# Three slots for block 1's diagonal products, quarter copies of W_in, and one cast moved to VectorE

## The chip, the cores and the metric

The kernel runs on one core of one Trainium2 chip. The metric is the device time of one execution in microseconds (us). The time stamps below are us from the start of the profiled span; a profile is one execution, and the span is some 1.8 us shorter than the time reported for it.

## The reference

```python
# causal depthwise convolution over the sequence, softmax-normalised weights per head, 7 taps
w = softmax(weight)                                   # [8 heads, 7]
out[b, s, h, :] = sum_k w[h, k] * x_pad[b, s + k, h, :]   # x: [8, 4096, 192]
# then a two-layer perceptron with exact GELU on the 32768 tokens
h = out.reshape(32768, 192) @ w_in                    # w_in: [192, 2048]
g = 0.5 * h * (1 + erf(h / sqrt(2)))
y = g @ w_out                                         # w_out: [2048, 192]
```

## The kernel before

The tokens go through in blocks: six of 256 columns, then blocks of 512, each for both halves of the tokens. Names used below: PE is TensorE, ACT is ScalarE, DVE is VectorE, POOL is GpSimd.

The 192 channels are held as three planes of 64. For blocks 0 and 1 the convolution is done on PE, as products with diagonal matrices accumulated in PSUM (`pconv`, 7 taps for each of four groups `kd`: planes 0 and 1, and two halves of plane 2). From block 2 on it is done on DVE. The evictions of block 1's products, that is the copies out of PSUM to `xc`, are on DVE. A part below is the share of one plane in the first products of a unit; `S_PCE` has counted two evictions of block 0 already, hence the 2:

```python
def wait_pc(e, n, p):               # block 1: parts 0, 1, 2 need 1, 3, 6 of the six evictions
    if n == 0: ...
    else:
        e.wait_ge(S_PCE, 2 + (1, 3, 6)[p])
```

DVE's program at the start, and PE's for block 0 (a "unit" is one call of `mm1`, 12 first-layer products that one GELU of ACT consumes; block 0 has units 0 to 7):

```python
for p in range(NP):                 # DVE
    trans(0, p)
conv_out(v, 0, 1)
conv_out(v, 0, 4)
dup(0)                              # copies of W_in to the other 64 partitions,
dup(1)                              # needed by units 4, 5, 6
for p in range(NP):
    trans(1, p)
dup(2)                              # twice as long as the others
for j in range(len(PIECES)):        # six evictions of block 1
    conv_out(v, 1, j)
# ... cut: transposes and taps of block 2 and on

behind = {                          # PE: block 1's diagonal products, each set in a slot behind a unit of block 0
    (0, 4): [(1, kd, k) for k in taps for kd in (0, 1)],
    (0, 5): [(1, kd, k) for k in taps for kd in (2, 3)],
}
def mm1(n, i):
    if u >= 2:
        t.wait_ge(S_GELU, u - 1)    # two PSUM buffers between PE and ACT
    if i == 0:
        if n in PC: wait_pc(t, n, NP - 2)
        else: t.wait_ge(S_CV, cvd(n))   # block 2 and on wait for DVE's convolution
    # ... cut: waits for W_in and its copies
    for cc in range(c):
        for p in range(NP):
            if n in PC and i == 0 and cc == 0 and p == NP - 1:
                wait_pc(t, n, p)    # the third part waits for all six evictions
            # ... cut: the products
```

The second layer of block 0 (`mm2`) starts behind block 1's first unit. I call the start of its first product the *hand-over*.

Of the kernel before, what the change touches and what calls it, by code (L numbers as in the profile page):

```python
# [11 lines left out]
def bass_lightweight_conv__then__act_gelu_exact_kernel(  # L12
# [9 lines left out]
    D2, F = moe_w_in.shape  # L22
# [10 lines left out]
    WS = [256] * 6 + [512] * ((HALF - 1536) // 512)  # L33
    PC = {0: 0, 1: 1}
# [7 lines left out]
    NP = D // 64  # L42
# [6 lines left out]
    HX = 8  # L49
    HF = HX - (KS - 1)  # L50
    XW = HX + TB
    HB = KS - 1
    HL = 32 * HB
    XB = HL + WS[0]
# [36 lines left out]
    for n in range(NB):  # L91
        k = 64 if n == 0 or M0 <= n < M1 else 16 * NG[n] if n < NB - 1 else 32 * NG[n]
# [10 lines left out]
    def sem(name):  # L103
        return es.enter_context(nc.semaphore(name))

    def ap(t, off, pat):
        return bass.AP(t, off, pat)

    with es:
        win = sbt("win", [128, NP * F], BF16)  # L110
# [14 lines left out]
        xTb = [sbt("xTb%d" % i, [128, NP * XB], BF16) for i in range(len(PC))]  # L125
        xin = [sbt("xin%d" % i, [128, TB // 32 * DQ], F32) for i in range(NX)]
        xT = [sbt("xT%d" % i, [128, NP * XW], F32) for i in range(2)]
# [18 lines left out]
        S_DG = sem("S_DG")  # L146
        S_HOT = sem("S_HOT")
        S_CAST = [sem("S_CAST%d" % i) for i in range(len(PC))]
        S_PC = sem("S_PC")
        S_PCE = sem("S_PCE")  # L150
        S_PCA = sem("S_PCA")
# [2 lines left out]
        S_TR = sem("S_TR")  # L154
# [50 lines left out]
        FQ = F // 8  # L205
# [256 lines left out]
        def _(v):  # L462
# [34 lines left out]

            def dup(s):

                v.wait_ge(S_WIN[s], 32)  # L500
                for hf in range(2):
                    v.tensor_copy(
                        ap(
                            win,
                            64 * (1 - hf) * NP * F + FH + FP[s],
                            [[NP * F, 64], [F, NP], [1, FP[s + 1] - FP[s]]],
                        ),
                        ap(
                            win,
                            64 * hf * NP * F + FP[s],  # L510
                            [[NP * F, 64], [F, NP], [1, FP[s + 1] - FP[s]]],
                        ),
                    ).then_inc(S_DUPE)

            def trans(n, p):
                w = WS[n]
                if p == 0:
                    if xin_at(n) > 0:
                        v.wait_ge(S_XIN[n % NX], xin_at(n))
                    if n >= 2 and n - 2 in PC:  # L520
                        wait_pc(v, n - 2, NP - 1)
                    elif n >= 2:
                        v.wait_ge(S_CV, cvd(n - 2))
                    if n >= 1:
                        v.wait_ge(S_HALO, HC[n])
                v.transpose(  # L526
                    ap(xT[n % 2], p * XW + HX, [[NP * XW, 128], [1, w]]),
                    ap(
                        xin[n % NX],
                        p,  # L530
                        [[TB // 32 * DQ, 128], [D if n == 0 else DQ, w // 32], [NP, 32]],
                    ),
                ).then_inc(S_TR)
# [45 lines left out]

            for p in range(NP):  # L580
                trans(0, p)
            conv_out(v, 0, 1)
            conv_out(v, 0, 4)
            dup(0)
            dup(1)
            for p in range(NP):
                trans(1, p)
            dup(2)
            for j in range(len(PIECES)):
                conv_out(v, 1, j)  # L590

# [17 lines left out]
        @block.scalar  # L609
        def _(a):  # L610
            a.activation(
                out=hot[:, 0:1], in_=nc.const_aps.tensor(0.0, (1, 1), F32), func=AF.Exp
            ).then_inc(S_ACTP)
            load(a, 0, (2, 3))
            a.wait_ge(S_ACTP, 1)
            a.wait_ge(S_PRO, 1)
            a.activation(
                out=wex[:, :],
                in_=wsb[:, :],
                func=AF.Exp,  # L620
                bias=wmx[:, 0:1],
                accum_out=wsm[:, 0:1],
            ).then_inc(S_ACTP)
            a.activation(
                out=hot[:, 1:2], in_=nc.const_aps.tensor(0.0, (1, 1), F32), func=AF.Gelu
            ).then_inc(S_HOT)
            a.wait_ge(S_PRO, 9)
            for p in range(NP):
                a.wait_ge(S_TR, p + 1)  # L629
                a.activation(  # L630
                    out=ap(xTb[0], p * XB + HL, [[NP * XB, 128], [1, WS[0]]]),
                    in_=ap(xT[0], p * XW + HX, [[NP * XW, 128], [1, WS[0]]]),
                    func=AF.Copy,
                ).then_inc(S_CAST[0])
            for j in PA:
                conv_out(a, 0, j)

            due = {(1, 6): [(0, 0)]}
            for m in range(NA):
                if m >= 1:  # L640
                    due[m + 1, NSL[m + 1] // 2] = [(m, 0)]
                due[m + 2, 0] = [(m, 1)]

            first = {}
            for n, at in ((4, (3, 5, 6)), (5, (3, 5, 6)), (6, (2, 3, 5))):
                for p in range(NP):
                    first[n - 2, at[p]] = (n, p)

            def first_tap(n, p):
                w = WS[n]  # L650
                a.wait_ge(S_TR, NP * n + p + 1)
                if p == 0:
                    a.wait_ge(S_CV, cvd(n - 2))
                a.activation(  # L654
                    out=acc[n % 2][:, p * TB : p * TB + w],
                    in_=ap(xT[n % 2], p * XW + HX, [[NP * XW, 128], [1, w]]),
                    func=AF.Copy,
                    scale=wcol[:, KS - 1 : KS],
                ).then_inc(S_K0)

            for n in range(NB):
                w = WS[n]
                for i in range(NSL[n]):
                    u = SL0[n] + i
                    c = NCH[n]
                    if (n, i) in first:
                        first_tap(*first[n, i])
                    for k in due.get((n, i), []):
                        evac(a, *k)
                    a.wait_ge(S_MM1, u + 1)  # L670
                    if i == 0 and n >= 2:
                        a.wait_ge(S_MM2, MMC[n - 1])
                    if M0 <= n < M1:

                        src = [[2 * TB, 128], [1, 2 * TB]]
                        dst = [[NF * 2 * TB, 128], [1, 2 * TB]]
                    else:

                        src = [[2 * TB, 128], [TB, 2], [128, 4], [1, 128]]
                        dst = [[NF * 2 * TB, 128], [128, 2], [256, 4], [1, 128]]  # L680
                    a.activation(  # L681
                        out=ap(gT[n % 2], i * c * 2 * w, dst),
                        in_=ap(hp[u % 2], 0, src),
                        func=AF.Gelu,
                    ).then_inc(S_GELU)

            for g in range(NG[NB - 1]):
                evac_half(a, g, 1)
                store_half(a, g, 1)

        @block.tensor
        def _(t):
            t.wait_ge(S_WARM, 1)
            for i in range(16):
                t.matmul(hp[1][:, 0:512], warm[:, 0:128], warm[:, :])  # L695

            def pconv(n, kd, k):

                p, ex, c0, w = kinds(n)[kd]
                if k == KS - 1:  # L700
                    t.wait_ge(S_CAST[PC[n]], p + 1)
                    if n == 0:
                        t.wait_ge(S_DG, 1)
                if k == KS - 2:
                    t.wait_ge(S_HALO, HC[n] + 2 + p if n == 0 else HC[n + 1])
                for hf in range(2):
                    ho = hf ^ ex
                    r = slice(64 * hf, 64 * hf + 64)
                    d0 = k * 64
                    x0 = p * XB + (32 * k if n == 0 else HF + k) + c0  # L710
                    ins = t.matmul(  # L711
                        bank(kd, slice(64 * ho, 64 * ho + 64), w),
                        dg[r, d0 : d0 + 64],
                        xTb[PC[n]][r, x0 : x0 + w],
                        start=(k == KS - 1),
                        stop=(k == 0),
                        tile_position=(64 * hf, 64 * ho),
                    )
                if k == 0:
                    ins.then_inc(S_PC)  # L720

# [4 lines left out]
            for kd in order:  # L726
                pconv(*seq[kd].pop(0))

            behind = {
                (0, 4): [(1, kd, k) for k in taps for kd in (0, 1)],  # L730
                (0, 5): [(1, kd, k) for k in taps for kd in (2, 3)],
            }

            def mm1(n, i):
# [8 lines left out]
                        t.wait_ge(S_CV, cvd(n))  # L743
                if n == 0 and i < 3:
                    t.wait_ge(S_WIN[i], 32)
                if n == 0 and 4 <= i < 7:
                    t.wait_ge(S_DUPE, 2 * (i - 4) + 2)
                for cc in range(c):
                    for p in range(NP):
# [170 lines left out]
```

## Time and profile before

| | before |
|---|---|
| time, first three runs | 683.58, 683.60, 684.46 us |
| profiled run: time, span | 683.38, 681.6 us |
| PE busy | 675.0 us, 99% |
| DVE, ACT busy | 561.0 and 537.3 us |

PE is busy for 99% of the span. The edits touch only what comes ahead of block 2, so what they change counts only if it reaches PE's first product of block 2. The prediction below shows most of the lines. In them, the third column is the engine, L760 is a first-layer product or its weight load, L711 a diagonal product, L791 a second-layer product of the first blocks, L681 a GELU, L193 a DVE eviction of the convolution, L502 a copy of W_in, L526 a transpose of x and L559 a tap of DVE's convolution. Three more lines are needed below, the start of block 0's transposes, the hand-over and the first product of block 2:

```profile
5.93 1.33 DVE L526 STREAM_TRANSPOSE xT<-xin 128x256 f32<-128x256 f32 x3 [0.68 <-DMA xin<-in_x_dram]
...
18.68 0.49 PE L791 MATMUL ob<-wout,gT 64*128 64x192 bf16 x8
...
29.18 0.83 PE L760 MATMUL hp<-xc,win 64*128 64x256 bf16 x12
```

### The profile page before, as it was taken

Reading aid. Unit: us, or ns where it says so; the run is one execution under the profiler, and the core shown is the slowest. Engines: PE = TensorE matmul, PEld = TensorE weight load, DVE = VectorE, ACT = ScalarE, POOL = GpSimd, SP = SyncE. Lnnn points to the kernel's source line nnn. Section 1 sums busy time; section 2 is a strip of 40 time slices with the busy share of each in tenths; the row PEclk is TensorE's granted clock in tenths of the full one; section 3 lists DMA queues with packets and bytes.
Section 4 is the critical chain, followed back from the end, with each engine's and each line's share of the span. In section 5 each row is a group of like instructions: output and inputs, shape, how many; then the busy total and the mean of one; then the engine's idle time right before and its main releaser. Section 6 shows DMA issues by size and latency. Waiting matters only on the chain.

```text
span 681.6 us, 27317 instructions
## 1 busy us (share of the span) xinstructions
PE 675.0 (99%) x12576; PEld 410.1 (60%) x12576; DVE 561.0 (82%) x904; ACT 537.3 (79%) x550; POOL 38.9 (6%) x57
## 2 busy tenths in 40 slices
PE   8999999999999999999999999999999999999998
PEld 4899655555555555555555555555555555555556
DVE  6899979888889888899888898888898888988611
ACT  6899988787787777787777788777878777878772
POOL 5026000000000000000000000000000000000000
PEclk9999999999999999999999999999999999999999
DMA  9446323234332244332244422334322434310123
GB/s 222 86 101 134 79 60 75 43 75 95 96 94 58 45 91 94 95 86 47 60 94 95 94 69 46 78 94 96 94 52 46 95 94 96 83 42 21 48 49 94
DMA packets 132994, 54.79 MB, mean 80 GB/s; under 512 B 126480, under 2 KB 132752, under 8 KB 132880
## 3 DMA queue, kind: packets, MB, share of 16 engines
q1 hardware_dynamic: 130960, 51.50, 32.5%
q8 instruction: 98, 1.61, 1.0%
q0 software_dynamic: 1248, 0.79, 0.9%
q10 hardware_dynamic: 672, 0.76, 0.4%
q14 instruction: 16, 0.13, 0.1%
HBM read 28.66 MB, written 25.17 MB: 79 GB/s over the span
## 4 chain that ended last, share of the span: by engine, by line
PE 96%; ACT 2%; DMA 1%; issue 0%; DVE 0%; SPq 0%; ACTq 0%
PE hp L760 48%; PE ob L824 43%; PE ob L791 6%; ACT gT L681 2%; DMA xin<-in_x_dram 1%; PE ob L711 0%; ACT xc L191 0%; ACT osb L269 0%; DVE osb L311 0%; DVE xT L526 0%; ACT xTb L630 0%; SPq L872 0%; DVE osb L280 0%; SPq L329 0%; ACTq L629 0%
## 5 line engine op out<-in xcount | busy, mean ns | idle before, releaser
L681 ACT ACTIVATE gT<-hp 128x1024 bf16<-128x1024 f32 x512 | 523.3, 1024 | 128.8 <-PE hp L760 125.5
L760 PE MATMUL hp<-xc,win 64*64 64x512 bf16 (+2 forms) x6048 | 419.5, 366 | 1.5 <-ACT gT L681 0.7
L824 PE MATMUL ob<-gT,wout 64*64 64x512 bf16 x5376 | 366.3, 376 | 0.0
L559 DVE SCALAR_TENSOR_TENSOR acc<-xT,wcol,acc 128x512 f32<-128x512 f32 (+1 forms) x495 | 314.1, 698 | 0.0
L760 PEld LDWEIGHTS hp<-xc,win 64*64 64x64 bf16 (+1 forms) x6048 | 189.9, 106 | 134.8 <-ACT gT L681 2.5
L824 PEld LDWEIGHTS ob<-gT,wout 64*64 64x64 bf16 x5376 | 172.3, 118 | 122.8
L311 DVE STREAM_TRANSPOSE osb<-ob 128x512 f32<-128x512 f32 x84 | 74.1, 885 | 100.8 <-PE ob L824 100.8
L526 DVE STREAM_TRANSPOSE xT<-xin 128x512 f32<-128x512 f32 (+1 forms) x105 | 78.6, 797 | 3.8 <-DMA xin<-in_x_dram 3.8
L559 DVE SCALAR_TENSOR_TENSOR xc<-xT,wcol,acc 128x512 bf16<-128x512 f32 (+1 forms) x99 | 65.0, 708 | 0.0
L447 POOL COPY xT<-xT 128x18 f32<-128x18 f32 x30 | 27.9, 930 | 505.2 <-DVE xT L526 482.9
L791 PE MATMUL ob<-wout,gT 64*128 64x192 bf16 x1024 | 52.9, 243 | 0.3
L791 PEld LDWEIGHTS ob<-wout,gT 64*128 64x128 bf16 x1024 | 44.9, 94 | 5.2 <-PE ob L791 0.6
L552 DVE TENSOR_SCALAR acc<-xT,wcol 128x512 f32<-128x512 f32 (+1 forms) x90 | 37.5, 474 | 1.1
L282 ACT ACTIVATE osb<-ob 128x192 f32<-128x192 f32 x4 | 1.3, 332 | 9.5 <-PE ob L791 9.5
L280 DVE COPY osb<-ob 128x192 f32<-128x192 f32 x4 | 1.4, 358 | 8.4 <-PE ob L791 8.4
L695 PE MATMUL hp<-warm 128*128 128x512 bf16 x16 | 5.1, 485 | 1.3 <-DVE warm L463 1.3
L269 ACT ACTIVATE osb<-ob 128x384 f32<-128x384 f32 x12 | 5.8, 486 | 0.0
L654 ACT ACTIVATE acc<-xT,wcol 128x256 f32<-128x256 f32 (+1 forms) x9 | 5.2, 575 | 0.0
L695 PEld LDWEIGHTS hp<-warm 128*128 128x128 bf16 x16 | 1.8, 119 | 4.0 <-issue 1.9
L384 POOL DMA_DIRECT2D win<-in_moe_w_in_dram x6 | 3.9, 658 | 0.8 <-POOLq L905 0.8
L711 PE MATMUL ob<-xTb,dg 64*64 64x256 bf16 (+1 forms) x112 | 3.2, 245 | 0.7 <-ACT xTb L630 0.7
L193 DVE CAST xc<-ob 64x256 bf16<-64x256 f32 (+3 forms) x8 | 2.8, 357 | 1.3 <-PE ob L711 1.1
(31 smaller groups left out, 22.4 us busy)
## 6 DMA issues: line engine op xcount, KB each, us to landing
out_dram<-osb SPq DMA_DIRECT2D x122, 192.0 KB, 3.1
xin<-in_x_dram SPq DMA_DIRECT2D x116, 192.0 KB, 4.1
xin<-in_x_dram SPq DMA_DIRECT2D x20, 96.0 KB, 4.2
woutf<-in_moe_w_out_dram SPq DMA_DIRECT2D x4, 384.0 KB, 6.2
win<-in_moe_w_in_dram POOLq DMA_DIRECT2D x4, 96.0 KB, 4.6
win<-in_moe_w_in_dram POOLq DMA_DIRECT2D x2, 192.0 KB, 5.1
out_dram<-osb SPq DMA_DIRECT2D x8, 48.0 KB, 1.9
out_dram<-osb ACTq DMA_DIRECT2D x4, 96.0 KB, 1.9
```

Of the source, the lines that this page charges most:

```text
L269: e.activation(out=dst, in_=src, func=AF.Copy).then_inc(S_EVA)
L311: v.transpose(ap(osb[m % 2], j, [[8 * C, 128], [C // 2, TB // 32], [NP, 32]]), bank(ring(m, j)),).then_inc(S_EV)
L447: g.tensor_copy(dst, src).then_inc(S_HALO)
L526: v.transpose(ap(xT[n % 2], p * XW + HX, [[NP * XW, 128], [1, w]]), ap(xin[n % NX], p, [[TB // 32 * DQ, 128], [D if n == 0 else DQ, w // 3 ...
L552: ins = v.tensor_scalar(a, src, wk, None, ALU.mult)
L559: ins = v.scalar_tensor_tensor(dst, src, wk, a, op0=ALU.mult, op1=ALU.add)
L654: a.activation(out=acc[n % 2][:, p * TB : p * TB + w], in_=ap(xT[n % 2], p * XW + HX, [[NP * XW, 128], [1, w]]), func=AF.Copy, scale=wcol[ ...
L681: a.activation(out=ap(gT[n % 2], i * c * 2 * w, dst), in_=ap(hp[u % 2], 0, src), func=AF.Gelu,).then_inc(S_GELU)
L695: t.matmul(hp[1][:, 0:512], warm[:, 0:128], warm[:, :])
L760: ins = t.matmul(hp[u % 2][fo : fo + fw, o : o + w], ap(win, f1, [[NP * F, 64], [2, fw]]), xc[n % 2][r, p * TB : p * TB + w], start=(p == ...
L791: ins = t.matmul(bank(bb[sub], w=C), gT[m % 2][r, c0 : c0 + 128], wout[r, CH[sub][i] * C : (CH[sub][i] + 1) * C], start=(ph == 0 and i == ...
L824: ins = t.matmul(bank(ring(m, j), slice(64 * h, 64 * h + 64), w), ap(wout, 64 * hf * NF * C + CH[h][i] * C + j, [[NF * C, 64], [NP, 64]],) ...
```

## The change

Its intent is to keep ACT fed in block 0: there, ACT stood idle 0.63 and 0.26 us ahead of two GELUs (I call such a gap a bubble). The prediction puts the first down to PE's diagonal products behind unit 4 and the second to a unit that waits for the long copy; the second reading did not hold, as the run with the old slots shows. Four edits:

```diff
-            for i in range(16):                      # warm products on PE
+            for i in range(12):
...
             for p in range(NP):                      # DVE
                 trans(0, p)
+            v.wait_ge(S_TR, NP)
+            v.tensor_copy(<xTb[0], plane 2>, <xT[0], plane 2>).then_inc(S_CASTV)
             conv_out(v, 0, 1)
             conv_out(v, 0, 4)
-            dup(0)
-            dup(1)
+            for s in range(3):                       # dup(s) is now a quarter, FQ columns
+                dup(s)
             for p in range(NP):
                 trans(1, p)
-            dup(2)
+            dup(3)
...
-            for p in range(NP):                      # ACT: casts of block 0
+            for p in range(NP - 1):
...
             behind = {
-                (0, 4): [(1, kd, k) for k in taps for kd in (0, 1)],
-                (0, 5): [(1, kd, k) for k in taps for kd in (2, 3)],
+                (0, 5): [(1, kd, k) for k in taps[:4] for kd in (0, 1)],
+                (0, 6): [(1, kd, k) for k in taps[4:] for kd in (0, 1)],
+                (0, 7): [(1, kd, k) for k in taps for kd in (2, 3)],
             }
...
-                if n == 0 and 4 <= i < 7:
+                if n == 0 and i >= 4:
                     t.wait_ge(S_DUPE, 2 * (i - 4) + 2)
```

(The diff is cut: the addresses of the copies and of the cast, and the semaphore waits that go with the cast, are left out or shortened.)

More of the change, by code (lines that the diff above doesn't have):

```diff
@@ L148, in bass_lightweight_conv__then__act_gelu_exact_kernel @@
         S_CAST = [sem("S_CAST%d" % i) for i in range(len(PC))]
+        S_CASTV = sem("S_CASTV")
         S_PC = sem("S_PC")
@@ L498, in dup @@
             def dup(s):
-                v.wait_ge(S_WIN[s], 32)
+                v.wait_ge(S_WIN[min(s, 2)], 32)
                 for hf in range(2):
@@ L504, in dup @@
                             win,
-                            64 * (1 - hf) * NP * F + FH + FP[s],
-                            [[NP * F, 64], [F, NP], [1, FP[s + 1] - FP[s]]],
-                        ),
-                        ap(
-                            win,
-                            64 * hf * NP * F + FP[s],
-                            [[NP * F, 64], [F, NP], [1, FP[s + 1] - FP[s]]],
-                        ),
+                            64 * (1 - hf) * NP * F + FH + FQ * s,
+                            [[NP * F, 64], [F, NP], [1, FQ]],
+                        ),
+                        ap(win, 64 * hf * NP * F + FQ * s, [[NP * F, 64], [F, NP], [1, FQ]]),
                     ).then_inc(S_DUPE)
@@ L581, in _ @@
                 trans(0, p)
+            v.wait_ge(S_TR, NP)
+            v.tensor_copy(
+                ap(xTb[0], (NP - 1) * XB + HL, [[NP * XB, 128], [1, WS[0]]]),
+                ap(xT[0], (NP - 1) * XW + HX, [[NP * XW, 128], [1, WS[0]]]),
+            ).then_inc(S_CASTV)
             conv_out(v, 0, 1)
             conv_out(v, 0, 4)
-            dup(0)
-            dup(1)
+            for s in range(3):
+                dup(s)
             for p in range(NP):
                 trans(1, p)
-            dup(2)
+            dup(3)
             for j in range(len(PIECES)):
@@ L700, in pconv @@
                 if k == KS - 1:
-                    t.wait_ge(S_CAST[PC[n]], p + 1)
+                    if n == 0 and p == NP - 1:
+                        t.wait_ge(S_CASTV, 1)
+                    else:
+                        t.wait_ge(S_CAST[PC[n]], p + 1)
                     if n == 0:
```

## The prediction

> **What bounds the kernel now.** I read the page first, then the list of waits, the chain of waits, and the timeline of the first 40 us, narrowed to single instructions where two events lie close.
>
> The page says that TensorE is the engine and that the rest of the chain is thin:
>
> ```profile
> PE 675.0 (99%) x12576; PEld 410.1 (60%) x12576; DVE 561.0 (82%) x904; ACT 537.3 (79%) x550; POOL 38.9 (6%) x57
> ...
> PE 96%; ACT 2%; DMA 1%; issue 0%; DVE 0%; SPq 0%; ACTq 0%
> ```
>
> The list of waits for PE alone has five rows, 3.2 us together, and all of them lie in the first 18 us. So everything that the change touches (warm-up, the convolution of blocks 0 and 1 as diagonal products on PE, the copies of W_in across the partition halves) lies in a preamble of about 20 us out of 681.6 us, and from there to the end PE issues back to back, apart from a ScalarE-paced stretch at 70 to 80 us. A shift of PE at 20 us therefore arrives at the end one for one, unless another wait takes it up in between. The question is whether the shift survives until PE is alone. This is the timeline, in four pieces:
>
> ```profile
> 13.79 1.99 DVE L502 COPY win<-win 64x1536 bf16<-64x1536 bf16 x2
> 13.89 0.96 PE L711 MATMUL ob<-xTb,dg 64*64 64x256 bf16 x28
> ...
> 15.65 1.02 ACT L681 ACTIVATE gT<-hp 128x1024 bf16<-128x1024 f32 x1 [0.63 <-PE hp L760]
> 15.81 2.29 DVE L193 CAST xc<-ob 128x256 bf16<-128x256 f32 x6
> ...
> 16.93 4.00 ACT L681 ACTIVATE gT<-hp 128x1024 bf16<-128x1024 f32 x4 [0.26 <-PE hp L760]
> ...
> 18.01 0.55 PEld L760 LDWEIGHTS hp<-xc,win 64*128 64x128 bf16 x12 [0.37 <-ACT gT L681]
> ...
> 19.65 1.35 DVE L526 STREAM_TRANSPOSE xT<-xin 128x256 f32<-128x256 f32 x3 [1.54 <-DMA xin<-in_x_dram]
> ...
> 27.77 1.26 DVE L559 SCALAR_TENSOR_TENSOR xc<-xT,wcol,acc 128x256 bf16<-128x256 f32 x3
> ...
> 29.14 0.58 PEld L760 LDWEIGHTS hp<-xc,win 64*128 64x128 bf16 x12 [0.15 <-issue]
> ```
>
> Columns are start, length, engine and group; the bracket is idle time before it and its releaser. To see: (a) the two GELUs with 0.63 and 0.26 us of idle ahead of them are the bubbles that the change is after: ScalarE starves in block 0 because PE does 28 diagonal products at 13.89 ahead of a first-layer unit, and because the next but one unit waits for the long copy on VectorE, which ends at 15.78. (b) The first unit of block 1 starts at 18.01, released by a GELU that ends at 17.96; VectorE's six evictions of block 1 end at 18.10, just in time for the unit's third part. (c) VectorE then idles 1.54 us until x of block 2 has landed at 19.62, and is busy without a break until it has finished block 2's convolution at 29.03. (d) PE's last second-layer product ahead of block 2 starts at 28.98, so by its spacing of 0.08 us the next could start at 29.06; it starts at 29.18. PE waits there for VectorE by 0.12 us. So two chains arrive at block 2 almost together: PE's from 18.01 and VectorE's from the DMA at 19.62.
>
> [...] the warm products start 0.43 us apart until 4.21 us and 0.215 us apart after that. [...] here the 64x256 eviction takes 424 ns, so the six are 2.29 us[...]. [...]
>
> **Part by part.**
>
> *12 warm products, not 16.* The 12th warm product started at 5.07 us and the first diagonal product waits for the first cast of x, at 7.02. Four fewer remove nothing from the path. PE's idle gap there grows from 0.71 to about 1.6 us[...]. Cost 0.
>
> *Third cast of block 0 on VectorE.* ScalarE's third cast took 0.42 us and ended at 7.71; VectorE's transposes end at 7.26, and its f32 op of this size (the tensor_scalar) takes 348 ns, so it ends near 7.65. It falls in VectorE's idle of 1.09 us ahead of its first eviction. ScalarE waits for PE until 8.01 anyway, then does four evictions back to back to 9.39, and these set the first unit. Worth 0.
>
> *Copies in quarters, three of the four ahead of block 1's transposes.* Quarter 2 needs the third load of W_in, landed at 10.70; VectorE gets to it at 10.87 and needs 2 x 0.45 us, to 11.8. The transposes wait for x until 12.41 anyway. Free. After the transposes (13.75) remain two copies of 768 columns, 0.42 us each undisturbed, up to twice that beside GpSimd: done at 14.7 to 15.4, not 15.78. VectorE would be ready for block 1's evictions 0.4 to 1.1 us earlier.
>
> *Diagonal products in three slots.* Products of planes 0 and 1 move from behind unit 4 to behind units 5 (16) and 6 (12), those of plane 2 from behind unit 5 to behind unit 7. The GELUs then run without bubbles: 0.63 + 0.26 = 0.89 us are gone, less a little, and the GELU of unit 6 ends near 17.1. But the evictions need finished products. Step by step: unit 5 follows the GELU of unit 3 (ends 13.99): 14.04 to 14.71. 16 products at 7 pairs of pairs per 0.80 us (28 in the trace from 13.89 to 14.69) are 0.46 us: 15.2. Unit 6 may start at 15.07 by its GELU, so at 15.25, to 15.9. 12 products: 0.34 us, finished with the drain of 0.27 us at about 16.45. So VectorE's evictions start at 16.45 and not at 15.81, and end at 16.45 + 2.29 = 18.75 and not at 18.10. Block 1's first unit waits for them (five evictions for its first two parts, all for the third): its third part starts at about 18.8, where it started at 18.24. With 8 of 12 products to go it hands over to the second layer at 18.8 + 0.44 = 19.24 instead of 18.68: **PE is 0.56 us later**, for the same work follows (about 10.4 us to block 2 with no wait that could take it up[...]).
>
> At block 2 PE would then be ready at 29.06 + 0.56 = 29.62; VectorE's chain from the DMA still ends at 29.03, so the 0.12 us wait is gone. Net 0.56 - 0.12 = +0.44 us, carried to the end: 683.6 + 0.44 = 684.0.
>
> **The rivals.**
>
> *The bubbles are worth their 0.89 us.* For it: they are real gaps on the engine that paces block 0, and block 1's first unit was released by a GELU. Against it: PE could then be ahead at block 2 by 0.8 us, but block 2 waits for VectorE, whose chain hangs on a DMA that nothing in the change touches (same queue, same order, issued at 10.53 to 12.62 without a wait for compute). At most the 0.12 us less a semaphore's delay could show: 683.5. A real gain would need x of block 2 to land earlier as well.
>
> *Everything is hidden.* If the products finish 0.4 us sooner than I reckon, the two arrivals at block 2 stay within a tenth and the time is 683.6.
>
> [...]
>
> [...] PE lost 0.34 us inside unit 7 in the trace with no releaser shown. In the changed kernel PE waits near there anyhow, so it should hide.
>
> **Range and chances.** My sum is +0.4; the scatter of the kernel before is 683.58 to 684.46, and the DMA landing can move both kernels by some tenths. I give 683.3 to 684.8, and 684.0 as the time. 2% would be 13.7 us, nearly the whole of the part touched, so within 2% is all but certain.
>
> **What would show it.** In the changed profile: GELUs of block 0 back to back from 10.1 to about 18.2 (bubbles gone); six copies of 64x768 ahead of block 1's transposes, two after; VectorE's six evictions starting at 16.3 to 16.6, having waited for PE; PE's wait inside block 1's first unit with VectorE as the releaser; block 2's first unit starting at about 29.6 with no wait for VectorE. I am wrong if block 2's first unit starts at 29.2 or earlier, if the evictions start before 16.0, or if x of block 2 lands at another time than 19.6.

Passages are cut out of the prediction where no trace or run of this case showed what they said of the hardware, among them a whole rival (684.6 to 685 us). No term of the sum went with them: it is still 0.56 - 0.12 = +0.44 us, and 683.6 + 0.44 = 684.0. Four points in it need a word:

- The cost of 0 for four warm products fewer is the author's estimate from the starts of the twelfth warm product (5.07 us) and the first diagonal product (7.02). That the products would keep their pace after a gap of 1.6 us instead of 0.71 was not shown at that point.
- "Up to twice that beside GpSimd" is an estimate from the kernel before: of the two equal 64x1536 copies, both beside casts of GpSimd, one took 0.68 us and the other 1.28. What made the second longer is not shown.
- The "drain of 0.27 us" is the length that the trace gives one diagonal product of 256 columns, 273 ns on average, with a modelled end. In the changed kernel's profile the evictions started 0.31 us after the start of the last of the 12 products (16.74 to 17.05).
- For the "semaphore's delay" the prediction has no figure of its own: in the trace 0.15 us lie between DVE's end at 29.03 and PE's first product of block 2 at 29.18.

## The result

The changed kernel took 684.25 us (median of 4 runs, 684.15 to 684.34), the kernel before 684.03 in the same rounds taken together with its first runs (683.58 to 685.49). The ratio of the fast runs is 1.0000, with a 95% interval from 0.9982 to 1.0017. A ratio here is the mean time of one kernel's fast runs over that of the other's of the same rounds, so it is not quite the ratio of the medians. The time lies in the predicted range and close to the predicted 684.0. That alone says little: the range also holds the time of the kernel before, so a change worth nothing would have ended in it too. What tests the reasoning is the timeline and the experiments.

The page of the changed kernel, first its busy times and then its chain of waits:

```profile
PE 674.3 (99%) x12572; PEld 406.8 (60%) x12572; DVE 561.5 (82%) x907; ACT 536.4 (79%) x549; POOL 38.7 (6%) x57
...
PE 96%; ACT 2%; DMA 1%; DVE 1%; issue 0%; SPq 0%; DVEq 0%; ACTq 0%
```

PE is the bound as before; a thin DVE share has appeared in the chain. This is the timeline of the changed kernel around the same events (start, length, engine and group, idle time before it and its releaser; L766, L716, L797, L683, L194, L503, L523 and L556 are now what L760, L711, L791, L681, L193, L502, L526 and L559 were):

```profile
6.30 1.34 DVE L523 STREAM_TRANSPOSE xT<-xin 128x256 f32<-128x256 f32 x3 [1.06 <-DMA xin<-in_x_dram]
...
14.15 0.87 DVE L503 COPY win<-win 64x768 bf16<-64x768 bf16 x2
...
15.17 0.63 PE L716 MATMUL ob<-xTb,dg 64*64 64x256 bf16 x16
...
16.49 0.52 PE L716 MATMUL ob<-xTb,dg 64*64 64x256 bf16 x12
16.61 1.02 ACT L683 ACTIVATE gT<-hp 128x1024 bf16<-128x1024 f32 x1 [0.30 <-PE hp L766]
...
17.05 2.29 DVE L194 CAST xc<-ob 128x256 bf16<-128x256 f32 x6 [2.03 <-PE ob L716]
...
17.82 1.02 ACT L683 ACTIVATE gT<-hp 128x1024 bf16<-128x1024 f32 x1 [0.19 <-PE hp L766]
...
19.40 0.61 PE L766 MATMUL hp<-xc,win 64*128 64x256 bf16 x8 [0.48 <-DVE xc L194]
...
19.85 0.49 PE L797 MATMUL ob<-wout,gT 64*128 64x192 bf16 x8
...
20.06 2.01 ACT L683 ACTIVATE gT<-hp 128x1024 bf16<-128x1024 f32 x2 [1.21 <-PE hp L766]
...
20.33 1.34 DVE L523 STREAM_TRANSPOSE xT<-xin 128x256 f32<-128x256 f32 x3 [0.99 <-DMA xin<-in_x_dram]
```

The reader is to see five things. The copies after block 1's transposes are down from 1.99 to 0.87 us, and DVE then has nothing to do for 2.03 us: its evictions wait for PE's 12 products at 16.49. The bubbles ahead of the GELUs shrank from 0.63 and 0.26 us to 0.30 and 0.19. The evictions end at 17.05 + 2.29, near 19.35, and the third part of block 1's first unit starts behind them at 19.40, with DVE named as releaser. The hand-over is at 19.85, where it was 18.68. And ACT has a new gap, of 1.21 us, ahead of block 1's first GELU, where it had none before (the line at 16.93 in the prediction runs through to 20.93): up to there ACT now idles 0.30 + 0.19 + 1.21 = 1.70 us instead of 0.89. In sum the idle time was not removed but moved, and it grew.

Not all of that 1.17 us is the change. In this execution the first input landed later: block 0's transposes began at 6.30, not at 5.93. Counted from there, the hand-over moved from 12.75 to 13.55 us, by 0.80.

At block 2 the changed kernel's timeline reads:

```profile
28.45 1.27 DVE L556 SCALAR_TENSOR_TENSOR xc<-xT,wcol,acc 128x256 bf16<-128x256 f32 x3
...
30.20 0.82 PE L766 MATMUL hp<-xc,win 64*128 64x256 bf16 x12
```

DVE ends block 2's convolution at 29.71, and PE comes half a microsecond later without a wait. The stretch from block 2's first product to the end is 652.43 us before and 652.40 after.

### The profile page after: what moved, and what is told of

Same layout as the page of the kernel before. It is cut to its first block, busy times and chain, and to the rows that moved or that the text cites. A ratio compares the mean times of both kernels' runs of the same rounds, so it can differ in the third digit from the quotient of the medians.

```text
span 682.6 us, 27312 instructions
## 1 busy us (share of the span) xinstructions
PE 674.3 (99%) x12572; PEld 406.8 (60%) x12572; DVE 561.5 (82%) x907; ACT 536.4 (79%) x549; POOL 38.7 (6%) x57
## 4 chain that ended last, share of the span: by engine, by line
PE 96%; ACT 2%; DMA 1%; DVE 1%; issue 0%; SPq 0%; DVEq 0%; ACTq 0%
PE hp L766 47%; PE ob L830 43%; PE ob L797 6%; ACT gT L683 2%; DMA xin<-in_x_dram 1%; PE ob L716 0%; DVE xc L194 0%; ACT xc L192 0%; ACT osb L270 0%; DVE osb L312 0%; DVE xT L523 0%; ACT xTb L632 0%; SPq L878 0%; DVE osb L281 0%; SPq L330 0%
## 5 line engine op out<-in xcount | busy, mean ns | idle before, releaser
L683 ACT ACTIVATE gT<-hp 128x1024 bf16<-128x1024 f32 x512 | 522.8, 1023 | 130.0 <-PE hp L766 126.7
L766 PE MATMUL hp<-xc,win 64*64 64x512 bf16 (+2 forms) x6048 | 418.9, 366 | 2.0 <-DVE xc L194 0.7
L556 DVE SCALAR_TENSOR_TENSOR acc<-xT,wcol,acc 128x512 f32<-128x512 f32 (+1 forms) x495 | 315.1, 706 | 0.2 <-ACT acc L656 0.2
L766 PEld LDWEIGHTS hp<-xc,win 64*64 64x64 bf16 (+1 forms) x6048 | 187.6, 106 | 137.0 <-ACT gT L683 2.5
L523 DVE STREAM_TRANSPOSE xT<-xin 128x512 f32<-128x512 f32 (+1 forms) x105 | 79.1, 816 | 2.7 <-DMA xin<-in_x_dram 2.7
L556 DVE SCALAR_TENSOR_TENSOR xc<-xT,wcol,acc 128x512 bf16<-128x512 f32 (+1 forms) x99 | 65.4, 720 | 0.0
L797 PE MATMUL ob<-wout,gT 64*128 64x192 bf16 x1024 | 52.2, 243 | 0.3
L797 PEld LDWEIGHTS ob<-wout,gT 64*128 64x128 bf16 x1024 | 43.7, 94 | 6.2 <-PE ob L797 0.6
L716 PE MATMUL ob<-xTb,dg 64*64 64x256 bf16 (+1 forms) x112 | 3.4, 247 | 1.9 <-ACT xTb L632 1.9
L194 DVE CAST xc<-ob 64x256 bf16<-64x256 f32 (+3 forms) x8 | 2.8, 357 | 2.9 <-PE ob L716 2.8
L716 PEld LDWEIGHTS ob<-xTb,dg 64*64 64x64 bf16 x112 | 2.5, 106 | 3.0 <-ACT xTb L632 2.4
```

Source lines behind the costliest of these rows:

```text
L523: v.transpose(ap(xT[n % 2], p * XW + HX, [[NP * XW, 128], [1, w]]), ap(xin[n % NX], p, [[TB // 32 * DQ, 128], [D if n == 0 else DQ, w // 3 ...
L556: ins = v.scalar_tensor_tensor(dst, src, wk, a, op0=ALU.mult, op1=ALU.add)
L683: a.activation(out=ap(gT[n % 2], i * c * 2 * w, dst), in_=ap(hp[u % 2], 0, src), func=AF.Gelu,).then_inc(S_GELU)
L716: ins = t.matmul(bank(kd, slice(64 * ho, 64 * ho + 64), w), dg[r, d0 : d0 + 64], xTb[PC[n]][r, x0 : x0 + w], start=(k == KS - 1), stop=(k ...
L766: ins = t.matmul(hp[u % 2][fo : fo + fw, o : o + w], ap(win, f1, [[NP * F, 64], [2, fw]]), xc[n % 2][r, p * TB : p * TB + w], start=(p == ...
L797: ins = t.matmul(bank(bb[sub], w=C), gT[m % 2][r, c0 : c0 + 128], wout[r, CH[sub][i] * C : (CH[sub][i] + 1) * C], start=(ph == 0 and i == ...
```

## The experiments

**Theory.** Block 2's first product starts at the later of two chains: PE's own, which is the hand-over plus the 10.34 us that PE then needs, and DVE's, which hangs on the landing of block 2's input. The changed kernel's slots delay PE's chain, because the evictions start only when the products of planes 0 and 1 are done. **Rivals:** the change is worth nothing and the two profiles differ only by when the inputs landed; the quarters, the cast or the shorter warm-up cost the time; PE's chain alone sets the end.

Eleven runs were made, each timed in five rounds (two of them repeat a kernel), and all gave correct results.

### The changed kernel again

No edit.

> The changed kernel once more, timed in five rounds beside the one before. My theory (block 1's first unit waits for VectorE's evictions, which start later because the diagonal products finish later): 0.4 to 0.7 us slower, ratio 1.0006 to 1.0010, and in the profile the second layer's first product 13.5 us after the start of block 0's transposes, as in the first profile of it (19.85 - 6.30 = 13.55) against 12.75 before (18.68 - 5.93). Rival (the two profiles differ because the inputs landed 0.4 us later in one of them, and the change is worth nothing): ratio 1.0000 within 0.0003, and the distance near 12.8.

Measured: 684.12 us (684.08 to 684.72) against 683.83 (683.49 to 685.27, 9 runs); ratio 1.0005, interval 0.9992 to 1.0017. The profile:

```profile
16.81 2.29 DVE L194 CAST xc<-ob 128x256 bf16<-128x256 f32 x6 [2.09 <-PE ob L716]
...
19.16 0.61 PE L766 MATMUL hp<-xc,win 64*128 64x256 bf16 x8 [0.48 <-DVE xc L194]
```

The same picture with inputs 0.25 us earlier. The hand-over is 13.56 us after the start of block 0's transposes (19.61 - 6.05), where the first profile had 13.55. So the delay by 0.8 us is the kernel's own and no accident of the inputs, against the first rival. The time difference of about 0.3 us is smaller than I expected here, and the interval includes 1.

### The two old slots in the changed kernel

```diff
-                (0, 5): ... taps[:4] ... (0, 1)
-                (0, 6): ... taps[4:] ... (0, 1)
-                (0, 7): ... taps ... (2, 3)
+                (0, 4): ... taps ... (0, 1)
+                (0, 5): ... taps ... (2, 3)
```

> The changed kernel with the diagonal products of block 1 back in the two slots of before (behind units 4 and 5); quarters, third cast on VectorE and 12 warm products stay. My theory: VectorE's evictions of block 1 start near 15.0 (when the copies are done) instead of 17.05 and end before the first unit of block 1 asks for them; GELU's bubble of about 0.6 us ahead of unit 5 comes back; the first second-layer product is again 12.7 us after block 0's transposes, block 2 waits again for VectorE, and the time is that of the kernel before within 0.2 us. Rival (the quarters or the cast cost the time): the distance stays at 13.5 us and the time 0.5 us above before.

Measured: 683.62 us (683.30 to 684.29), ratio to before 0.9997 (0.9984 to 1.0009). Its timeline:

```profile
15.00 2.29 DVE L194 CAST xc<-ob 128x256 bf16<-128x256 f32 x6 [0.46 <-PE ob L716]
...
15.77 1.02 ACT L683 ACTIVATE gT<-hp 128x1024 bf16<-128x1024 f32 x1 [0.63 <-PE hp L765]
...
17.05 3.96 ACT L683 ACTIVATE gT<-hp 128x1024 bf16<-128x1024 f32 x4 [0.26 <-PE hp L765]
...
18.80 0.49 PE L796 MATMUL ob<-wout,gT 64*128 64x192 bf16 x8
```

The evictions start at 15.00, the bubbles of 0.63 and 0.26 us are back, and the hand-over is at 12.75 us after block 0's transposes, exactly as before. The bubble of 0.26 us is there although all copies were done at 14.55, so it was not the long copy that made it. In the kernel before, too, the copy had ended (15.78) ahead of unit 6 (16.06), which followed the last of the 28 diagonal products behind unit 5 without a wait. The mean of its five runs, 683.69, is 0.55 us below the mean of the changed kernel's five on the same chip, 684.24. The slots are what costs, not the quarters, the cast or the warm-up. One detail of my expectation failed: block 2 did not wait for DVE. In this execution the input of block 2 landed early (transposes at 19.44), DVE was done at 28.83, and PE came without a wait at 29.14 = 18.80 + 10.34.

### The three slots alone in the kernel before

```diff
-                (0, 4): ... (0, 1)     -> as in the change:
+                (0, 5), (0, 6): ... (0, 1);  (0, 7): ... (2, 3)
```

> The kernel before with the three slots (behind units 5, 6 and 7) as its only edit. My theory: this alone makes the loss: evictions of block 1 start only when the 12 products behind unit 6 are done, near 17, unit 6 may moreover wait for the long copy until 15.8, so the distance from block 0's transposes to the first second-layer product is 13.5 us or up to 0.3 more, and the time 0.4 to 0.9 us above before. Rival (the slots pay for themselves by GELUs without bubbles): distance 12.8 or less, time equal.

Measured: 685.01 us (684.53 to 685.81), ratio 1.0014 (1.0000 to 1.0028), that is 1.1 us between the means; all five runs are slower than the changed kernel's median. The profiled run was its slowest, and block 1's input landed late in it (transposes at 13.68). Its timeline:

```profile
17.20 0.83 PE L761 MATMUL hp<-xc,win 64*128 64x256 bf16 x12 [1.14 <-DVE win L502]
...
18.52 2.29 DVE L193 CAST xc<-ob 128x256 bf16<-128x256 f32 x6 [1.47 <-PE ob L711]
```

Unit 6 waits 1.14 us for the long copy, which ends at 17.05, and only then come the 12 products and the evictions. So without the quarters the slots cost more; with the quarters this wait is gone. The sign is as expected and the size is above my range; how much of it is the late input I can't separate in this one profile.

### The three slots one unit earlier

```diff
-                (0, 5), (0, 6): ... (0, 1);  (0, 7): ... (2, 3)
+                (0, 4), (0, 5): ... (0, 1);  (0, 6): ... (2, 3)
```

> The changed kernel with its three slots one unit earlier (behind units 4, 5 and 6). My theory: the products of planes 0 and 1 are done near 15.8 instead of 17.0, the evictions run from 15.9 to 18.2, the first unit of block 1 starts at about 17.8 and hands over near 18.6, at most 0.1 us earlier than before; block 2 still waits for VectorE, whose chain starts with the landing of x, so the time is that of before within 0.2 us, not better. Rival (the hand-over sets the end, no other wait catches it): a hand-over earlier by some tenths shows in full at the end.

Measured: 684.07 us (683.25 to 684.72), ratio 1.0002 (0.9989 to 1.0014). The profiled run was the slowest of the five, and again block 1's input was late:

```profile
13.69 1.36 DVE L523 STREAM_TRANSPOSE xT<-xin 128x256 f32<-128x256 f32 x3 [1.23 <-DMA xin<-in_x_dram]
...
30.54 0.83 PE L766 MATMUL hp<-xc,win 64*128 64x256 bf16 x12 [0.19 <-DVE xc L556]
```

PE waited 0.26 us for the casts of block 1 at its first slot, and the hand-over came at 19.83 instead of my 18.6, so the profile does not test the hand-over. It does show the second chain: PE was ready at 19.83 + 10.34 = 30.17, DVE ended block 2's convolution at 30.39, and PE started at 30.54. This run and the one before it made me ask about the landing of block 1's input, which I had taken as fixed.

### Block 1's input late, in the kernel before and in the changed one

```diff
-            load(sp, 1)
             for i in range(4):
+                if i == 1:
+                    load(sp, 1)
                 ...                     # quarter i of W_out
```

> The kernel before with the load of x for block 1 issued after the first quarter load of W_out, so that it lands about 1.1 us later (near 13.5 instead of 12.4). Theory S (in the kernel before, the copies after block 1's transposes and the products behind unit 4 hang on this landing, and this is why its times scatter up to 685.5): the transposes, the long copy's end, unit 6 and the hand-over to the second layer all move by 1.1 us, block 2 starts near 30.1 to 30.3 and the time rises by 0.8 to 1.1 us, to 684.5 to 685. Rival: block 1's inputs have slack and nothing moves: time within 0.2 us of before.

> The changed kernel with the same late load. Theory S: the products of block 1 stand behind unit 5 and later, where there is 0.9 us or so of slack to the casts, and only 0.9 us of copies follow the transposes; the hand-over stays at 13.5 to 13.8 us after block 0's transposes and the time at 684.1 to 684.4, equal to or below the kernel before with the same late load. Rival: it moves like the other by 1 us, to 685.2.

Measured: before with the late load 685.04 us (684.23 to 687.30, 6 runs), ratio 1.0016 (1.0002 to 1.0030); changed with the late load 684.46 (684.42 to 684.92), ratio 1.0006 (0.9993 to 1.0019). The kernel before with the late load:

```profile
14.03 1.33 DVE L526 STREAM_TRANSPOSE xT<-xin 128x256 f32<-128x256 f32 x3 [3.18 <-DMA xin<-in_x_dram]
...
15.07 1.36 PE L711 MATMUL ob<-xTb,dg 64*64 64x256 bf16 x28 [1.03 <-POOL xTb L213]
...
17.23 1.02 ACT L681 ACTIVATE gT<-hp 128x1024 bf16<-128x1024 f32 x1 [2.13 <-PE hp L760]
```

and the changed kernel with it:

```profile
13.95 1.35 DVE L523 STREAM_TRANSPOSE xT<-xin 128x256 f32<-128x256 f32 x3 [2.16 <-DMA xin<-in_x_dram]
...
14.99 1.05 PE L716 MATMUL ob<-xTb,dg 64*64 64x256 bf16 x16
...
16.84 1.02 ACT L683 ACTIVATE gT<-hp 128x1024 bf16<-128x1024 f32 x1 [0.86 <-PE hp L766]
```

In both the transposes start near 14.0, about 1.5 us late, where I had reckoned with 13.5; that is part of why both hand-overs moved further than I expected. The old slot behind unit 4 stalls PE by 1.03 us and ACT by 2.13; the new slot behind unit 5 is reached when the casts are nearly there, and ACT idles 0.86 us. Counted from block 0's transposes, the hand-over moves by 1.57 us in the kernel before (12.75 to 14.32) and by 0.55 in the changed one (13.56 to 14.11). In the means of the runs the late load costs the kernel before 1.1 us (684.09 to 685.22) and the changed one 0.3 us (684.24, 684.57 here). One of the six late runs of the kernel before, 687.30, stands far out; without it the 1.1 us would be 0.7. So the changed kernel gives up about 0.8 us of hand-over and buys tolerance to a late input. Whether the slots or the quarters buy it was not separated: in the kernel before with the late load, the evictions started at 17.42, just behind the end of the long copy at 17.39.

### Two slots, behind units 5 and 6

```diff
-                (0, 5), (0, 6): ... (0, 1);  (0, 7): ... (2, 3)
+                (0, 5): ... taps ... (0, 1)
+                (0, 6): ... taps ... (2, 3)
```

> The changed kernel with two slots, all products of planes 0 and 1 behind unit 5 and those of plane 2 behind unit 6. My theory: evictions start near 15.9 to 16.2 and end near 18.3, the hand-over comes 12.7 to 12.9 us after block 0's transposes, as before, and the time is that of before at its fastest (683.5 to 683.8), since block 2 waits for VectorE anyway, without the slow runs of before. Rival: the evictions are not what counts, distance 13.5 and 684.1.

Measured: 683.49 us (683.37 to 683.91), ratio 0.9992 (0.9980 to 1.0004). Evictions start at 15.89, the hand-over is at 12.66 us after block 0's transposes, 0.9 us earlier than in the changed kernel. The profiled run was the slowest of its five; in it DVE's chain was late (block 2's transposes from 20.23, done with the convolution at 29.62):

```profile
29.76 0.83 PE L765 MATMUL hp<-xc,win 64*128 64x256 bf16 x12 [0.38 <-ACT gT L683]
```

The view names a GELU as the releaser, one that ended at 29.70. By the code this unit needs only the GELU before that one, which ended at 28.07, so it was DVE that PE waited for. PE was ready near 29.2: its last second-layer products ahead of block 2 began at 28.47, and in the profiles without a wait block 2 follows such a start after 0.74 or 0.75 us. (From the hand-over PE took some 0.2 us more than 10.34 here, since the unit behind it waited for a GELU.) So PE's lead of half a microsecond bought nothing there.

### Block 2's input late in the changed kernel

```diff
+            load(sp, 3)
             load(sp, 2)
-            load(sp, 3)
```

> The changed kernel with the loads of x for blocks 2 and 3 exchanged, so that block 2's lands 0.7 to 1.5 us later. Theory of two chains: in the changed kernel PE reaches block 2 about 0.5 us after VectorE has finished its convolution; VectorE's chain now ends 0.7 to 1.5 us later, so block 2 waits for VectorE and the time rises by 0.2 to 1.0 us above the changed kernel's, and the stretch from block 2's first product to the end stays at 652.4 us. Rival (PE's chain alone sets the end): no change.

Measured: 685.17 us (684.70 to 685.97), ratio 1.0015 (1.0003 to 1.0027), about 1 us above the changed kernel (684.12 in the first call).

```profile
31.00 0.83 PE L766 MATMUL hp<-xc,win 64*128 64x256 bf16 x12 [0.83 <-DVE xc L556]
```

The hand-over is as in the changed kernel, 13.55 us after block 0's transposes, but now PE waits 0.83 us for DVE, whose transposes of block 2 started at 21.48 (before: 19.65; the changed kernel's profiles: 20.33 and 19.95). DVE ended at 30.86, and from 31.00 to the end there are 652.43 us. That PE's chain alone sets the end is ruled out.

### Two slots with block 1's input late

The edits of the two experiments above together.

> The kernel with two slots behind units 5 and 6, with block 1's x loaded after the first quarter of W_out. Block 1's transposes then start near 14.0. If the slot behind unit 5 gives the slack that the changed kernel had: products start near 15.2, evictions end near 18.8, hand-over 13.3 us after block 0's transposes, time 683.7 to 684.3, below both kernels with the same late load (685.0 and 684.5). If the slot's slack is too small: hand-over at 13.8 or later and 684.5 or more.

Measured: 685.07 us (684.23 to 685.41), ratio 1.0012 (0.9999 to 1.0024). The profile fell on the fastest of the five: evictions from 16.81, hand-over 13.47 us after block 0's transposes, where I had expected 13.3. The median is above the 683.7 to 684.3 that I expected. Two of the five runs (684.23 and 684.33) are as good as the changed kernel with the late load, the other three (685.07 to 685.41) are as slow as the kernel before with it. So two slots behind 5 and 6 keep only a part of the changed kernel's tolerance; what happened in the slow runs is open, since they weren't profiled.

### Warm-up and cast put back in the changed kernel

```diff
-            for i in range(12):
+            for i in range(16):
...                               # and the third cast of block 0 on ACT again
```

> The changed kernel with 16 warm products and the third cast of block 0 back on ScalarE. My theory: both were worth nothing; GELU starts 4.15 to 4.2 us after block 0's transposes as in all profiles so far, the hand-over stays at 13.55 us after them, time 684.1 within 0.2. Rival (they bought or cost something on the way to the first unit): the distance from block 0's transposes to the first GELU changes by 0.1 us or more.

Measured: 684.22 us (683.90 to 684.52), ratio 1.0004 (0.9990 to 1.0017). The first GELU starts 4.17 us after block 0's transposes (changed kernel: 4.16 and 4.17), and the hand-over 13.56 us after them. Taken together the two edits were worth nothing, as predicted; they were not tested one by one.

### Two slots again

No further edit.

> The kernel with slots behind units 5 and 6 again, on the same chip as these two and the kernel before: 683.4 to 683.9, with all runs within 0.6 us, ratio to before 0.9990 to 0.9998.

Measured: 683.40 us (683.32 to 684.01), ratio 0.9993 (0.9981 to 1.0006); the spread of 0.69 us is slightly more than I had said. This profile again fell on a slow run (683.93): PE stood 0.69 us inside unit 7 with no releaser shown, the hand-over came at 13.24 us, a unit then waited for a GELU, and block 2 started at 29.76.

The ten runs of this version have a mean of 683.60 us, the nine runs of the changed kernel 684.25 and the 33 runs of the kernel before 684.05. The two-slot version is thus the fastest of the three by 0.45 and 0.64 us of mean; I work out standard errors of 0.13 and 0.11 us, treating all the runs as independent although they come from several chips. It is 0.1% at best, and each interval against the kernel before still includes 1.

## Why the prediction was right

**Where the time is decided.** Confirmed, and more exactly than I could know. In all thirteen profiles the stretch from block 2's first product to the end is 652.40 to 652.44 us. A shift at block 2 arrives at the end one for one.

**Two chains at block 2.** Confirmed. In seven of the thirteen profiles block 2 starts 10.34 or 10.35 us after the hand-over, with DVE done earlier. In the kernel before and three experiments (the early slots, the first run with two slots, block 2's input late) DVE was last, and PE starts 0.14 or 0.15 us after DVE's end. In the other two, both with two slots, PE was last but took 10.43 and 10.66 us, because a unit behind the hand-over waited for a GELU.

**Warm products and cast, worth 0.** Confirmed, as a pair, by putting them back. PE's gap ahead of the first diagonal product grew to 1.86 us (predicted 1.6; in this run the input was 0.37 us later) and no slow products followed: the 56 diagonal products of block 0 took 1.69 us, before 1.68; DVE's cast took 295 ns (predicted 348).

**Quarter copies.** Confirmed: all six early copies were done ahead of block 1's transposes, the last two took 0.42 us each, done at 15.02 (predicted 14.7 to 15.4). What the prediction had wrong here is its reading (a) that the long copy made the second bubble: with quarters and the old slots the bubble of 0.26 us stayed, and so did the hand-over at 12.75 us. With the old slots the earlier copies were worth nothing in these profiles; with the new slots and no quarters, unit 6 waited 1.14 us.

**The slots make the evictions late.** The mechanism is confirmed by the run with the old slots; the size was too small. From the start of block 0's transposes, I predicted evictions at 10.52 us (16.45 - 5.93) and they came at 10.75 and 10.76. The term of the sum that was too small is the turn from a unit to diagonal products: I let PE go on at its usual step of 0.11 us, and the trace has 0.20 us from the last start of one kind to the first of the other, at all three turns ahead of the evictions (14.97 to 15.17, 15.53 to 15.73, 16.29 to 16.49). My sum had 0.20 us for the second of them only, so the first and the third were 0.09 us too short each, most of the 0.23 us. The turns are also a part of why the bubbles didn't vanish but remained at 0.30 and 0.19 us. The hand-over was then 0.80 us late, not 0.56. A slip without effect: the first two parts of block 1's first unit need three of its evictions, not five (five is what `S_PCE` must count, with two of block 0 in it); the third part, which sets the hand-over, needs all six, as I had it.

**Net +0.44 us.** Counted from block 0's transposes, block 2 started at 23.90 us in both profiles of the changed kernel and at 23.25 before: +0.65. The medians say only +0.2 to +0.3 (684.25 against 684.03, 684.12 against 683.83), and the intervals don't exclude 0. Part of the reason is the step in which I took the landing of the inputs as the same for both kernels. It isn't the same from run to run, and the two kernels don't react alike: with block 1's input late, the kernel before loses 1.1 us (0.7 without its one far run) and the changed one 0.3. The kernel before also has slow runs (683.31 to 685.49 over 33) that pull its average towards the changed kernel's, whose nine runs lie between 684.08 and 684.72. That these slow runs are late landings of block 1's input is likely but not shown, as only one execution of the unedited kernel before was profiled, a fast one.

**The rival of a gain of 0.89 us** was rightly set aside. Its mirror image was seen in the two-slot version, whose hand-over was early and whose PE then waited for DVE.

**The signs it named.** The evictions waited for PE, DVE was the releaser inside block 1's first unit, and block 2 started without a wait for DVE, all as foretold. The GELUs did not run back to back. In absolute time the evictions started at 17.05 and block 2 at 30.20 (predicted 16.3 to 16.6 and about 29.6), partly by the late inputs of that execution. That the median came so near 684.0 is in part luck: the kernel before, taken as 683.6, had a median of 684.03 in the same rounds, so the difference of the medians was 0.22 us, not 0.44.

**x of block 2 at 19.6** was wrong as a fixed time, and the prediction had named this as a sign of being wrong: DVE's transposes of block 2, which follow that landing, started at 20.33 and 19.95 in the changed kernel. It did no harm, because there DVE's chain still ends 0.5 to 0.6 us ahead of PE's.

## What to carry to other kernels

Before you remove a bubble, find the point at which the chains meet for the last time and ask which one arrives later there: a bubble upstream of a meeting is worth at most the slack of the other chain. Work moved later to fill one engine's gap delays whatever is made from it; here ACT's gaps in block 0 shrank by 0.40 us and a new one of 1.21 us opened at block 1. Compare the distance between two events in a profile when times differ by less than their scatter, and ask whether an edit changes the best run or the tolerance to a late input.

## What else the traces show

- In the changed kernel first-layer products (64 by 128 tiles) step pairwise by 0.11 us, and between them and diagonal products of 256 columns (64 by 64 tiles) lie 0.20 us. The cause was not tested.
- In the changed kernel the 64x768 copies beside GpSimd's casts took 419 and 421 ns, as alone, while the casts beside them took 514 and 931 ns instead of about 400 and 822. In each of these overlaps it was the operation that began later that took longer: those copies began 0.03 and 0.05 us ahead of a cast; in the kernel before, the first 64x1536 copy (0.68 us) began 0.03 us ahead of one, which took 648 ns instead of 402, and the second (1.28 us) began 0.09 us behind one. From the start of the first to the end of the second it was 1.99 us there, and 1.99 and 2.00 in two other profiles (the slots alone; the kernel before with the late load). The order was never changed by itself, so it is not shown to be the cause.
- The landing of the same load scatters: the transposes that follow block 1's input started at 12.29 to 13.69 us in profiles with an unchanged order of loads.
- In the changed kernel PE stood idle for 1.86 us after 4.3 us of warm products, and the 56 diagonal products behind this gap took 1.69 us, where they took 1.68 behind a gap of 0.71 in the kernel before.
